# Block products (seven instead of eight) in the last matrix product of a fused attention and MLP kernel, with lam moved into W2

## The chip, the cores and the metric

The kernel runs on one core of a Trainium2 chip. A core has five engines with a queue each, worked through in order: TensorE (PE; its weight loads are listed apart, as PEld), VectorE (DVE), ScalarE (ACT), GpSimd (POOL) and SyncE (SP, which here only issues transfers). The engines meet at semaphores. SBUF is the working memory; PSUM, of eight banks, is where TensorE writes its sums. The metric is the device time of one execution in microseconds (us), the median of several runs.

## What is computed

The reference gives attention within blocks after a learned mixing of the blocks, and then a residual MLP. Batch 4, 8 heads, 768 rows, head size 64, 8 blocks of 96 rows, so C = 512 channels; hidden size 2048.

```python
P = sort_net                                   # (4, 8, 8, 8); five rounds of
P = exp(P - max);  P = P / rowsum;  P = P / colsum
k_sorted = einsum('bhij,bhjcd->bhicd', P, k_b) # v likewise
attn = softmax(q_b @ k_sorted^T / 8)           # within each block of 96 rows
x = attn @ v_sorted                            # then heads side by side: (4, 768, 512)

a1  = alpha1 * x + beta1
tok = einsum('ts,bsd->btd', w_tok, a1)
u   = x + lam * tok
a2  = alpha2 * u + beta2
ch  = relu(a2 @ w_ch1) @ w_ch2
out = u + lam * ch
```

## The kernel before

**Stages.** Everything is written out as one order of instructions for each engine (the class `Engine`, whose `fixed` keeps the order of the program on its engine). After a start-up for batch 0, a loop runs over the four batches b and over two halves hf of 384 rows each. I write such a half as (b, hf). A half has two phases:

- the **h phase**: sixteen units h0 to h15. A unit (`h_unit`, lines 725 to 741) is four matmuls of 128x384 that make 128 hidden rows of `a2 @ w_ch1`, and one ScalarE relu into `hTa` (m below 12) or `hTb`.
- the **c phase**: three output tiles kk = 0 to 2 of 128 rows and 512 columns, each in four parts of four matmuls (`ch_unit`, lines 760 to 780): twelve parts, c0 to c11. VectorE multiplies a finished tile by `lamB` (line 777), GpSimd adds `u` (line 778; VectorE in the last half), and two transfers write it out. The very last tile is split into 256, 128 and 128 columns (`last_out`, line 743).

**Work put between.** The table `at` (line 859) holds what is run after each unit or part: `put(b, hf, "h", m, f)` puts f after unit m. In the stretch of batch p the attention of batch p + 1 is put there (lines 882 to 927):

- `mix_v` and `mix_k` (lines 535 and 550) mix the blocks of the next values and keys on TensorE, and ScalarE or VectorE copies them out. `bounce_v` and `back_v` send the values through DRAM into `Vs`.
- `q_cross` (line 515) transposes the queries by transfers.
- `score` (line 419), for one head pair and one half of the blocks: eight small matmuls into a PSUM tile, and one ScalarE exp of 96x768 (`et`). Units go in pairs, written s0,s1 and so on to s6,s7.
- `pv` (line 479): eight matmuls into a PSUM tile `x_ps`, then on VectorE a reciprocal (`rcb`) and a multiplication into `x`. The two operations that make `a1` (`first_affine`, line 443) go to the list `late`, and `flush` (line 506) issues them. Pairs are written pv0,pv1 to pv6,pv7.
- `mix_matrix` (line 376) makes the mixing matrices of a later batch: one small matmul (`repv_ps`) and six VectorE operations, of which the first (`sel`) reads that PSUM tile.
- `moe_tok` (line 698): six matmuls of 128x512 (`tok_ps`), VectorE's multiplication by lam into `toktmp` and `u16`, and `u32` on GpSimd. `moe_cross` transposes `u16` by transfers, and `moe_affine` makes `a2T` from it.

**Buffers.** PSUM has two pools. `psA` has two buffers (of two banks) for `score`, `pv`, `mix_v`, `mix_k` and `mix_matrix`; `psB` has four buffers (of one bank) for `h_ps`, `ch_ps` and `tok_ps`. Each pool hands its buffers out in turn: a tile waits until the one that had its buffer (two tiles back in `psA`, four in `psB`) has been read. So TensorE waits where the reader of such a tile is late.

**Batch 0.** In (0,0) `w_tok` is still being transposed: `prep_wtok(ks, 1)` runs after unit ks, and its copy is VectorE's for even ks and ScalarE's for odd ones (line 871). `first_affine` for batch 0 runs after units 0 to 3 (line 877) and `moe_tok(0, 3 .. 5)` after units 7 to 9 (line 869).

Of the kernel before, what the change touches and what calls it, by code (L numbers as in the profile page):

```python
# [16 lines left out]
def kernel(  # L17
# [87 lines left out]
    lam1 = att.tile([1, C], FT, name="lam1", tag="toktmp", bufs=2)  # L105
    bet1 = att.tile([1, C], FT, name="bet1", tag="ost", bufs=2)
    nc.sync.dma_start(lam1[:], moe_lam.rearrange("(o c) -> o c", o=1))
    nc.sync.dma_start(bet1[:], moe_beta1.rearrange("(o c) -> o c", o=1))

    KT0 = att.tile([128, H4, NB, 128], F16, name="kT0", tag="kT", bufs=2)  # L110
    VD = att.tile([128, D, 64], F16, name="vd", tag="kT", bufs=2)
    Vs = [const([128, H * NB, GRP], F16, f"Vs_{n}") for n in range(2)]
    q8 = moep.tile([128, H4, 12 * D], F16, name="q8", tag="u16", bufs=1)
# [39 lines left out]
    for half in range(2):  # L153
        t_ = att.tile([128, 3, S], F16, name="wt16", tag=("mixed", "qn")[half], bufs=1)
        for lo, n in ((0, 96), (TAIL, 32)):
            pool.dma_start(
                t_[lo // 6:lo // 6 + n],
                moe_w_tok[lo + 3 * half * n:lo + 3 * (half + 1) * n, :].rearrange("(tt p) s -> p tt s", p=n),
            )
        wt16.append(t_)  # L160
        if half == 0:
            pool.memset(VD[:, :, HB:64], 0.0)
            pool.memset(
                KT0[:].rearrange("p g i (th t) -> p (g i th) t", th=2)[:, :, HB:64].bitcast(FT), 0.0
            )
# [4 lines left out]
    W1p = const([128, CT, HID], BF, "W1p")  # L170
    W2p = const([128, HT, C], BF, "W2p")
    w1v = moe_w_ch1.rearrange("(ci p) n -> p ci n", p=128)
# [230 lines left out]
    def v_mix(b, n, ps, eng):  # L403
        ps = ps([128, 8, 64], FT, "v_ps")
        fill(ps[:].rearrange("p d x -> p (d x)"), 1 - n % 2)
        for s in range(8):
            for th in range(2):
                d = (s + 4 * th) % 8
                r = slice(th * 64, th * 64 + 64)
                pe.matmul(  # L410
                    ps[r, d, :], VD[r, n * 8 + d, :],
                    bigV[b][r, :, :].rearrange("p h i -> p (h i)"), start=True, stop=True,
                )
        eng(Vs[0][:, :, n * 8:(n + 1) * 8], ps[:].rearrange("p d x -> p x d"))

# [3 lines left out]
    def score(b, g, hf, ps):  # L419
# [3 lines left out]
        for ii in range(4):  # L423
# [3 lines left out]
            for h2 in range(2):  # L427
# [4 lines left out]
                )  # L432
        tag, bufs = (("ost", "toktmp")[hf], 2) if (b, g) == (0, 3) else ("et", 6)
        et = att.tile([128, 2, 4, BLK], F16, name="et", tag=tag, bufs=bufs)
# [18 lines left out]
    def pv_first(g):  # L453
        if g == 0:
            x_of[0] = moep.tile([128, 8, C], F16, name="x128", tag="x128", bufs=2)
        ps = psa([128, 2, 512], FT, "x_ps")[:, :, 0:480].rearrange("p a (k d) -> p a k d", d=80)
        for i in range(NB):
            for h2 in range(2):
                et = ets[(0, g, i // 4)][:].rearrange("p a i t -> p (a i t)")
                lo = (4 * h2 + i % 4) * BLK  # L460
                w = min(128, 8 * BLK - lo)
                val = Vs[0][:, (2 * g + h2) * NB + i, 0:D + 1]
                if i < 6:
# [15 lines left out]
    def pv(b, g, hf):  # L479
        if g == 0 and hf == 0:  # L480
            x_of[b] = moep.tile([128, 8, C], F16, name="x128", tag="x128", bufs=2)
            a1_of[b] = moep.tile([128, 8, C], F16, name="a1", tag="a1", bufs=1)
        ps = psa([128, 2, 512], FT, "x_ps")[:].rearrange("p a (k d) -> p a k d", d=128)
        et = ets[(b, g, hf)][:].rearrange("p a i t -> p (a i t)")
        for ii in range(4):
            for h2 in range(2):
                lo = (4 * h2 + ii) * BLK
                w = min(128, 8 * BLK - lo)
                pe.matmul(
                    ps[0:w, h2, ii, 0:D + 1], et[0:BLK, lo:lo + w],  # L490
                    Vs[b % 2][0:BLK, (2 * g + h2) * NB + 4 * hf + ii, 0:D + 1], start=True, stop=True,
                )
# [13 lines left out]
    def flush():  # L506
        while late:
            late.pop(0)()

    def tails(x, lo, hi, eng):  # L510
# [24 lines left out]
    def mix_v(b, n, eng):  # L535
        if n == 0:
            mixed[b] = att.tile([128, HB, D], F16, name="mixed", tag="mixed", bufs=1)
        ps = psa([128, 2, 512], FT, "mix_ps")
# [37 lines left out]
    def back_v(b):  # L576
        sp.dma_start(Vs[b % 2][0:BLK, :, 0:D], vscr[b].rearrange("x t d -> t x d"))

# [136 lines left out]
    def moe_affine(b, hf):  # L715
        for ci in range(CT):
            affine(b, hf, ci, uT_of[(b, hf)][:, ci, :], dve)

    uT_of = {}

    hT_of = {}

    h_of = {}

    def h_part(b, hf, m, cis):
        if (b, hf) not in hT_of:
            hTa = moep.tile([128, 12, 384], BF, name="hTa", tag="hTa", bufs=1)
            hTb = moep.tile([128, HT - 12, 384], BF, name="hTb", tag="hTb", bufs=1)
            hT_of[(b, hf)] = [hTa[:, m, :] if m < 12 else hTb[:, m - 12, :] for m in range(HT)]
        if cis[0] == 0:  # L730
# [11 lines left out]

    def last_out(hT, cps, kk, kt):
        for n, (lo, hi) in enumerate(((0, 256), (256, 384), (384, 512))):
            c = slice(lo, hi)
            w = hi - lo
            if n:
                cps = psb([128, w], FT, "ch_ps")
                for m in range(HT):
                    pe.matmul(  # L750
                        cps[:], hT[m][:, kk * 128:(kk + 1) * 128], W2p[:, m, c],
                        start=(m == 0), stop=(m == HT - 1),
                    )
            ost = att.tile([128, C // 2], FT, name="ost", tag=("toktmp", "ost")[n % 2], bufs=2)
            dve.tensor_tensor(ost[:, 0:w], cps[:, 0:w], lamB[:, c], ALU.mult)
            dve.tensor_tensor(ost[:, 0:w], ost[:, 0:w], u_of[B - 1][kt][:, c], ALU.add)
            sp.dma_start(out[B - 1, kt * 96:(kt + 1) * 96, c], ost[0:96, 0:w])
            nc.scalar.dma_start(out[B - 1, TAIL + kt * 32:TAIL + (kt + 1) * 32, c], ost[96:128, 0:w])

    def ch_unit(b, hf, kk, part=(0, HT)):  # L760
# [4 lines left out]
        cps = ch_of[0]  # L765
        w = C // 2 if b == B - 1 and kt == NT - 1 else C
        for m in range(*part):
            pe.matmul(
                cps[:, 0:w], hT[m][:, kk * 128:(kk + 1) * 128], W2p[:, m, 0:w],
                start=(m == 0), stop=(m == HT - 1),  # L770
            )
        if part[1] < HT:
            return
        if b == B - 1 and kt == NT - 1:
            return last_out(hT, cps, kk, kt)
        ost = att.tile([128, C], FT, name="ost", tag="ost", bufs=2)
        dve.tensor_tensor(ost[:], cps[:], lamB[:], ALU.mult)
        (dve if b == B - 1 and hf == 1 else pool).tensor_tensor(ost[:], ost[:], u_of[b][kt], ALU.add)
        act_out(out[b, kt * 96:(kt + 1) * 96, :], ost[0:96, :])
        act_out(out[b, TAIL + kt * 32:TAIL + (kt + 1) * 32, :], ost[96:128, :])  # L780

    ch_of = {}
# [10 lines left out]
    prep_scales()  # L793
    dve.tensor_copy(Vs[0][:, :, D:GRP], mgap[:].unsqueeze(2).to_broadcast([128, H * NB, GRP - D]))
    kp0 = k_turn(0, 0, psb)
# [59 lines left out]
    load_q(1)  # L855
    pool.memset(Vs[1][0:BLK, :, D:GRP], 1.0)
    pool.memset(Vs[0][0:BLK, :, D:GRP], 1.0)

# [23 lines left out]
    for b in range(1, B):  # L882
        p = b - 1
        if b == 1:
            for n in range(3):
                put(0, 0, "h", 13 + n, lambda n=n: mix_v(1, n, dve.tensor_copy))
                put(0, 0, "c", 3 + 3 * n, lambda n=n: mix_k(1, n, ((act.copy, dve.tensor_copy)[n % 2],) * 4))
            put(0, 0, "h", 15, lambda: bounce_v(1))
# [8 lines left out]
        else:  # L897
# [9 lines left out]
            for (kind, n), at_ in zip(  # L907
                pairs, ((0, "h", 15), (0, "c", 1), (0, "c", 3), (0, "c", 6), (0, "c", 8), (0, "c", 11), (1, "h", 1), (1, "h", 4)),
            ):
                if kind == "p":  # L910
                    put(p, at_[0], at_[1], at_[2] + 1, flush)
                for i in range(2):
                    f = (lambda b=b, n=n + i: score(b, n // 2, n % 2, psa)) if kind == "s" else (lambda b=b, n=n + i: pv(b, n // 2, n % 2))
                    put(p, *at_, f)
        put(
            p, 1, "h", 15 if b == 1 else 8, lambda b=b: tails(a1_of[b], 0, C, dve.tensor_copy),
            lambda b=b: tails(x_of[b], 0, C, dve.tensor_copy),
        )
        put(p, 1, "h", 4, lambda b=b: moe_start(b))
        for kt in range(3):  # L920
            put(p, 1, "c", 4 if b == 1 else kt, lambda b=b, kt=kt: moe_tok(b, kt, psb))
        put(p, 1, "c", 4 if b == 1 else 2, lambda b=b: moe_cross(b, 0))
        put(p, 1, "c", 8 if b == 1 else 6, lambda b=b: moe_affine(b, 0))
        for kt in range(3):
            put(b, 0, "h", 2 * kt, lambda b=b, kt=kt: moe_tok(b, 3 + kt, psb))
        put(b, 0, "h", 4, lambda b=b: moe_cross(b, 1))
        put(b, 0, "c", 4, lambda b=b: moe_affine(b, 1))

# [11 lines left out]
    for b in range(B):  # L940
        for hf in range(2):
            for m in range(HT):
                if b or hf or m > 2:
                    h_unit(b, hf, m)
                    run(b, hf, "h", m)
            for kk in range(3):
                for part in range(4):
                    ch_unit(b, hf, kk, (4 * part, 4 * part + 4))
                    run(b, hf, "c", 4 * kk + part)

# [29 lines left out]
```

## Time and profile before

| what | value |
|---|---|
| median of 3 runs | 263.56 us (263.21 to 263.74) |
| the profiled execution | 263.49 us, of it a span of 261.7 us from the first to the last instruction |
| TensorE clock granted | 0.999 of full |
| waits of TensorE listed by the table of waits | 4.5 us, the longest of them 1.2 us |
| idle time of VectorE until a `ch_ps` tile was done | 54.6 us in 16 waits |
| idle time of ScalarE until an `h_ps` tile was done | 53.8 us in 75 waits |
| GpSimd adding `u` to output tiles | 26.6 us busy, 21 times, 1268 ns each |

One table by stage reads busy time in each stretch of the span (us). The stretches are (1,0), (1,1), (2,0), (2,1), (3,0) and (3,1), cut where a phase or an attention pair ends:

| stretch | length | PE | DVE | ACT | POOL |
|---|---|---|---|---|---|
| 102.4 to 130.6 | 28.2 | 28.20 | 14.66 | 14.34 | 13.34 |
| 130.6 to 158.9 | 28.3 | 28.30 | 17.90 | 18.75 | 11.74 |
| 158.9 to 186.8 | 27.9 | 27.90 | 13.43 | 14.23 | 8.78 |
| 186.8 to 212.5 | 25.7 | 25.70 | 16.16 | 9.10 | 8.74 |
| 212.5 to 237.1 | 24.6 | 24.60 | 8.33 | 7.84 | 8.78 |
| 237.1 to 261.7 | 24.6 | 21.01 | 5.48 | 7.84 | 1.27 |

A listed matmul time includes its drain and overlaps the next, so the cost of a matmul is read from the distance between starts, not from the busy time of one.

### The profile page before, as it was taken

The page shows a single profiled execution, that of the slowest core. Times are in us where ns is not written, and L with a number is a line of the kernel's source. Part 1 is how long each engine was busy: PE and PEld are TensorE (multiplying, and loading weights), DVE is VectorE, ACT ScalarE, POOL GpSimd, SP SyncE. Part 2 cuts the span into 40 slices and gives each one's busy share as a digit, 9 for nine tenths or more (in the row PEclk, how much of TensorE's full clock was granted, in tenths as well). Part 3 has the DMA queues.
Part 4 walks back from the last instruction along what each step waited for, and adds up shares of the span by engine and source line. Part 5 has one row for each costly group of instructions (what it writes and reads, how often), then busy time and mean ns, then how long its engine had stood idle before and what let it go on. Part 6 is the DMA issues. An engine that isn't in the chain of part 4 may idle for free.

```text
span 261.7 us, 5406 instructions
## 1 busy us (share of the span) xinstructions
PE 253.1 (97%) x2179; PEld 140.2 (54%) x2179; DVE 153.8 (59%) x345; ACT 133.8 (51%) x242; POOL 100.2 (38%) x105
## 2 busy tenths in 40 slices
PE   8998799999999999999999999999999999999994
PEld 3456565555556455555565454555565445545554
DVE  6796857987658984613988643407894554051024
ACT  3568666224787539474276288573373014504700
POOL 8759304501382084612860554501302746032000
PEclk9999999999999999999999999999999999999999
DMA  6999999998979957960899859901110332112012
GB/s 101 208 206 186 206 207 213 204 147 188 159 152 183 133 125 181 130 108 3 167 178 179 121 122 170 135 20 40 46 38 0 63 93 67 23 40 80 0 43 80
DMA packets 67533, 31.04 MB, mean 119 GB/s; under 512 B 56675, under 2 KB 63219, under 8 KB 67509
## 3 DMA queue, kind: packets, MB, share of 16 engines
q0 software_dynamic: 26352, 15.34, 42.3%
q1 hardware_dynamic: 41012, 15.30, 34.3%
q8 instruction: 17, 0.28, 0.4%
q10 hardware_dynamic: 144, 0.07, 0.1%
q14 instruction: 8, 0.06, 0.1%
HBM read 32.79 MB, written 8.65 MB: 158 GB/s over the span
## 4 chain that ended last, share of the span: by engine, by line
PE 82%; DMA 10%; POOL 5%; DVE 2%; issue 1%; ACT 0%; POOLq 0%
PE ch_ps L65 32%; PE h_ps L65 30%; PE tok_ps L65 10%; DMA W2p<-in_moe_w_ch_dram 6%; DMA v<-in_v_dram 4%; PE x_ps L65 2%; PE sc_ps L65 2%; DVE a L65 2%; PE kmix_ps L65 2%; PE mix_ps L65 1%; POOL W1p L65 1%; POOL vd L65 1%; POOL k L65 1%; PE qt_ps L65 1%; POOL brow L65 0%
## 5 line engine op out<-in xcount | busy, mean ns | idle before, releaser
L65 PE MATMUL h_ps<-a2T,W1p 128*128 128x384 bf16 x512 | 91.8, 326 | 0.1
L65 ACT ACTIVATE hTa<-h_ps 128x384 bf16<-128x384 f32 x96 | 46.7, 493 | 54.0 <-PE h_ps L65 53.8
L65 PE MATMUL ch_ps<-W2p,hTa 128*128 128x512 bf16 (+2 forms) x312 | 69.0, 363 | 0.0
L65 PEld LDWEIGHTS <-W1p 128*128 128x128 bf16 x512 | 48.3, 98 | 32.3 <-issue 0.3
L65 POOL TENSOR_TENSOR ost<-ost,u 128x512 f32<-128x512 f32 x21 | 26.6, 1268 | 80.2 <-DVE ost L65 53.2
L65 DVE TENSOR_TENSOR ost<-ch_ps,lamB 128x512 f32<-128x512 f32 (+2 forms) x26 | 16.8, 648 | 54.6 <-PE ch_ps L65 54.6
L65 PEld LDWEIGHTS <-hTa 128*128 128x128 bf16 x312 | 28.7, 98 | 28.9
L65 POOL TENSOR_TENSOR u<-toktmp,x 128x512 f32<-128x512 f32 x18 | 29.6, 1650 | 32.1 <-DVE toktmp L65 32.1
L65 ACT ACTIVATE et<-sc_ps 96x768 f16<-96x768 f32 (+1 forms) x32 | 24.8, 808 | 18.9 <-PE sc_ps L65 18.9
L65 PE MATMUL tok_ps<-a,w_tokT 128*128 128x512 f16 x126 | 30.3, 379 | 0.1
L65 ACT CAST kT<-kmix_ps 64x512 f16<-64x512 f32 x32 | 22.9, 717 | 10.1 <-PE kmix_ps L65 9.8
L65 DVE TENSOR_TENSOR toktmp<-tok_ps,lamB 128x512 f32<-128x512 f32 x21 | 14.5, 690 | 20.0 <-PE tok_ps L65 18.6
L65 PE MATMUL ch_ps<-W2p,hTb 128*128 128x512 bf16 (+2 forms) x104 | 25.0, 363 | 0.0
L65 PEld LDWEIGHTS <-w_tokT 128*128 128x128 f16 x126 | 12.2, 98 | 14.0 <-DVE a L65 0.5
L65 ACT ACTIVATE hTb<-h_ps 128x384 bf16<-128x384 f32 x32 | 15.7, 490 | 7.5 <-PE h_ps L65 7.2
L65 POOL DMA_DIRECT2D qn<-in_q_dram x18 | 16.0, 910 | 6.4 <-DMA raw<-in_v_dram 6.4
L65 DVE TENSOR_TENSOR u<-toktmp,x 128x512 f16<-128x512 f32 (+1 forms) x24 | 17.0, 719 | 0.7
L65 DVE TENSOR_TENSOR x<-x_ps,rcb 96x512 f16<-96x512 f32 x24 | 16.5, 687 | 0.8
L65 PEld LDWEIGHTS <-et 96*128 96x128 f16 (+4 forms) x288 | 11.9, 100 | 5.5 <-DVE x L65 1.6
L65 PEld LDWEIGHTS <-hTb 128*128 128x128 bf16 x104 | 9.6, 98 | 9.6
L65 PE MATMUL x_ps<-Vs,et 96*128 96x65 f16 (+4 forms) x288 | 13.0, 195 | 1.7 <-DVE x L65 0.9
L65 DVE TENSOR_TENSOR a<-x,alphaB 96x512 f16<-96x512 f16 (+1 forms) x28 | 13.8, 491 | 0.0
(118 smaller groups left out, 230.1 us busy)
## 6 DMA issues: line engine op xcount, KB each, us to landing
out_dram<-ost SPq DMA_DIRECT2D x23, 192.0 KB, 2.3
raw<-in_v_dram POOLq DMA_DIRECT2D x6, 384.0 KB, 8.1
raw<-in_k_dram POOLq DMA_DIRECT2D x6, 384.0 KB, 9.9
qn<-in_q_dram POOLq DMA_DIRECT2D x18, 128.0 KB, 11.0
vscr<-mixed SPq DMA_DIRECT2D x6, 384.0 KB, 5.2
Vs<-vscr SPq DMA_DIRECT2D x3, 768.0 KB
W1p<-in_moe_w_ch_dram POOLq DMA_DIRECT2D x4, 512.0 KB, 11.5
W2p<-in_moe_w_ch_dram POOLq DMA_DIRECT2D x4, 512.0 KB, 17.3
```

Source lines behind the costliest of these rows:

```text
L65: ins = getattr(self.eng, name)(*args, **kwargs)
```

## The change

1. **Block products.** In batches 1 to 3 tile 0 of each half stays as it was, and tiles 1 and 2 are made together by `ch_pair`. Rows, hidden size and columns are each cut in two, so there would be eight products of 128x1024 by 1024x256; seven suffice, each of eight matmuls of 128x256. Three sums of the hidden rows (`block_sums`) and four of the weights (`block_weights`) replace the eighth. Three PSUM tiles px, py, pz hold the running sums and are read between the products: VectorE adds their parts into the outputs in eight operations of 128x256 (`add_out`). In the last half the pair comes first and tile 0 last, in 256, 128 and 128 columns.
2. **lam in W2.** `scale_weights` multiplies 64 lam into W2 in four VectorE operations (128x2048 each) in (0,0); an output is then one VectorE operation, `ps / 64 + u`. GpSimd's additions to the outputs are gone.
3. **Types and buffers.** W2, `hTa` and `hTb` are f16 instead of bf16 and hold eight units each; four `ost` buffers instead of two; one `Vs` and one `x128` instead of two; `mixed` shares a buffer with the sums, or for batch 3 with `qn`.
4. **Places.** The pairs of `score` and `pv` move from h15, c1, c3, c6, c8, c11 and h1, h4 of the next half to h7, h10, h12, h15, c1, c4, c10 and h1. `first_affine` is flushed at h13, c6, c8 and h3. `moe_tok(b, 0 .. 2)` for b above 1 moves from c0, c1, c2 to h13, h14, h15. For b = 1, `mix_v` and `mix_k` are copied by ScalarE alone. `moe_affine(b, 1)` moves to ScalarE for b of 1 and more.

The core of the diff:

```diff
@@ h_part, ch_unit, new functions @@
+            hTa, hTb = (
+                moep.tile([128, HK, 384], F16, name=n, tag=n, bufs=1) for n in ("hTa", "hTb")
+            )
...
-        ost = att.tile([128, C], FT, name="ost", tag="ost", bufs=2)
-        dve.tensor_tensor(ost[:], cps[:], lamB[:], ALU.mult)
-        (dve if b == B - 1 and hf == 1 else pool).tensor_tensor(ost[:], ost[:], u_of[b][kt], ALU.add)
+        ost = att.tile([128, C], FT, name="ost", tag="ost", bufs=4)
+        add_out(ost[:], cps[:], u_of[b][kt])
...
+    def scale_weights(g):
+        if g == 0:
+            lam16 = lam_of[0] = att.tile([128, C], F16, name="lam16", tag="ost", bufs=4)
+            dve.tensor_scalar(lam16[:], lamB[:], GAIN, 0.0, op0=ALU.mult, op1=ALU.add)
+        w = W2p[:, 4 * g:4 * g + 4, :]
+        dve.tensor_tensor(w, w, lam_of[0][:].unsqueeze(1).to_broadcast([128, 4, C]), ALU.mult)
+
+    def add_out(dst, ps, other):
+        dve.scalar_tensor_tensor(dst, ps, 1.0 / GAIN, other, op0=ALU.mult, op1=ALU.add)
...
+        dst, x, y = ((t1, b12, b11), (t2, b22, t1), (t3, b22, b12), (t4, b21, t2))[n // 2]
+        dve.tensor_tensor(dst, x, y, ALU.subtract)
...
+    def block_sums(b, hf, part, k1=1, k2=2):
...
+        r = slice(part * HK // 2, (part + 1) * HK // 2)
+        dve.tensor_tensor(sm[:, 0, r, :], ha[:, r, c2], hb[:, r, c2], ALU.add)
+        dve.tensor_tensor(sm[:, 1, r, :], sm[:, 0, r, :], ha[:, r, c1], ALU.subtract)
+        dve.tensor_tensor(sm[:, 2, r, :], hb[:, r, c1], sm[:, 1, r, :], ALU.subtract)
+        if part:
+            dve.tensor_tensor(ha[:, :, c2], ha[:, :, c1], ha[:, :, c2], ALU.subtract)
...
+        px = psb([128, c], FT, "px")[:]
+        product(px, lambda j: ha[:, j, c1], lambda j: W2p[:, j, left], True)
+        o1 = att.tile([128, C], FT, name="ost", tag="ost", bufs=4)
+        add_out(o1[:, left], px, u1[:, left])
+        step()
+        py = psb([128, c], FT, "py")[:]
+        product(py, lambda j: hb[:, j, c1], lambda j: W2p[:, HK + j, left], True)
+        add_out(o1[:, left], py, o1[:, left])
...
+        step()
+        pz = psb([128, c], FT, "pz")[:]
+        product(pz, lambda j: sm[:, 0, j, :], lambda j: TW["a"][:, 0, j, :], True)
+        o2 = att.tile([128, C], FT, name="ost", tag="ost", bufs=4)
+        add_out(o2[:, right], pz, u2[:, right])
+        step()
+        product(px, lambda j: sm[:, 1, j, :], lambda j: TW["a"][:, 1, j, :], False)
+        add_out(o1[:, right], px, u1[:, right])
+        step()
+        product(pz, lambda j: sm[:, 2, j, :], lambda j: W2p[:, HK + j, right], False)
+        add_out(o1[:, right], pz, o1[:, right])
...
+        step()
+        product(py, lambda j: hb[:, j, c2], lambda j: TW["b"][:, 1, j, :], True)
+        add_out(o2[:, left], py, u2[:, left])
+        step()
+        product(px, lambda j: ha[:, j, c2], lambda j: TW["b"][:, 0, j, :], False)
+        for n, d in enumerate((right, left)):
+            add_out(o2[:, d], px, o2[:, d])
...
@@ places @@
-                pairs, ((0, "h", 15), (0, "c", 1), (0, "c", 3), (0, "c", 6), (0, "c", 8), (0, "c", 11), (1, "h", 1), (1, "h", 4)),
+                pairs, ((0, "h", 7), (0, "h", 10), (0, "h", 12), (0, "h", 15), (0, "c", 1), (0, "c", 4), (0, "c", 10), (1, "h", 1)),
...
+            put(p, 0, "h", 13, flush)
+            put(p, 0, "c", 6, flush_one)
+            put(p, 0, "c", 8, flush_one)
+            put(p, 1, "h", 3, flush)
...
+    for g, m in enumerate((3, 12, 13, 14)):
+        put(0, 0, "h", m, lambda g=g: scale_weights(g))
+    for n, at_ in enumerate(((0, 1, "h", 13), (0, 1, "h", 14), (0, 1, "h", 15), (0, 1, "c", 11)) + tuple((1, 0, "h", 5 + i) for i in range(4))):
+        put(*at_, lambda n=n: block_weights(n))
+    for b in range(1, B):
+        for hf in range(2):
+            put(b, hf, "h", 11, lambda b=b, hf=hf: block_sums(b, hf, 0))
+            put(b, hf, "h", 15, lambda b=b, hf=hf: block_sums(b, hf, 1))
...
+            for kk in range(1 if b else 3):
                 for part in range(4):
                     ch_unit(b, hf, kk, (4 * part, 4 * part + 4))
-                    run(b, hf, "c", 4 * kk + part)
+                    step()
+            if b:
+                ch_pair(b, hf, step)
+                step()
```

Each `step()` runs the work put at the next c place, so in batches 1 to 3 c0 to c3 follow the parts of tile 0 and c4 to c10 follow the seven products.

## Prediction, written before the result was known

> **What bounds the kernel now.** First the page's busy shares and the chain that ended last:
>
> ```profile
> span 261.7 us, 5406 instructions
> ...
> PE 253.1 (97%) x2179; PEld 140.2 (54%) x2179; DVE 153.8 (59%) x345; ACT 133.8 (51%) x242; POOL 100.2 (38%) x105
> ...
> PE 82%; DMA 10%; POOL 5%; DVE 2%; issue 1%; ACT 0%; POOLq 0%
> ```
>
> From some 44 us on the chain is TensorE's own queue; the other engines wait for it. TensorE's waits, of the table of waits, are as good as none in the loop (all lie in the start-up), so nothing there can be won but its own work:
>
> ```profile
> PE x_ps L65 <- DVE x L65: 0.9, 2, 0.4
> ...
> PE sc_ps L65 <- ACT et L65: 0.3, 1, 0.3
> ```
>
> Then the timeline, for the price of a matmul by its columns (start, length, and here the distance between starts), and for the spacing on ScalarE and VectorE:
>
> ```profile
> 250.96 2.75 PE L65 MATMUL ch_ps<-W2p,hTa 128*128 128x512 bf16 x12
> ...
> 254.41 1.47 PE L65 MATMUL ch_ps<-W2p,hTa 128*128 128x256 bf16 x12
> ...
> 256.16 0.83 PE L65 MATMUL ch_ps<-W2p,hTa 128*128 128x128 bf16 x12
> ```
>
> ```profile
> 173.38 0.49 ACT L65 ACTIVATE hTb<-h_ps 128x384 bf16<-128x384 f32 x1 [0.16 <-PE h_ps L65]
> 173.77 1.50 ACT L65 ACTIVATE et<-sc_ps 96x768 f16<-96x768 f32 x2
> ...
> 178.55 0.19 DVE L65 RECIPROCAL rcb<-x_ps 96x8 f32<-96x8 f32 x1
> ...
> 178.78 0.69 DVE L65 TENSOR_TENSOR x<-x_ps,rcb 96x512 f16<-96x512 f32 x1
> ```
>
> A tile of sixteen 512-column matmuls takes 254.41 - 250.96 = 3.45 (215.6 ns each), of 256 columns 256.16 - 254.41 = 1.75 (109.4 ns), and each loads its own weights; six f16 matmuls of `tok_ps` start 1.30 before what follows them, so f16 is as fast as bf16. ScalarE follows a relu with an exp after 0.39, an exp with the next after 0.69; relu's result is there 0.49 after its start, exp's 0.81. A relu starts 0.20 after its last matmul. A `pv` tile holds VectorE for 0.24 + 0.61, and is read 0.93 after `rcb` starts.
>
> **What is won.** Two tiles cost 32 x 215.6 = 6.90; seven products 56 x 109.4 = 6.13. 0.77 by six pairs: **-4.6**. At the end one operation stands for two of 0.29 behind the last matmul; the nearest form (SCALAR_TENSOR_TENSOR, 128x384, 618 ns) against TENSOR_TENSOR on the slope 292, 424, 690 ns makes it some 0.35: **-0.2**. GpSimd's 26.6 us were behind TensorE and win nothing.
>
> The Trainium skill, page "TensorE: Matmul & The Clock Gate", section "Back-to-back issue gap", speaks against the change: it says that in a stream of weight load and matmul both set the spacing, measured at 81 ns for 128 columns and 131 ns for 512. An estimate from it by a straight line (98 ns at 256) makes a pair 5.5 instead of 4.2 us, 7.8 lost over six pairs. The rows above (55.6, 109.4, 215.6 ns) are proportional to the columns, and they decide.
>
> **What VectorE gets.** 16-bit TENSOR_TENSOR from SBUF takes 0.42 at 512 and 0.55 at 768 (0.53 ns an element), so 0.42 for 512, 0.69 for 1024, 1.23 for 2048. The other end is the slope of the 32-bit rows, 1.04 ns: 0.69, 1.22, 2.28. I take the first, since those rows are of the same kind, with a broadcast operand too. `add_out` at 256: 0.42 (TENSOR_TENSOR) to 0.62 (the 384 row), taken as 0.48. Per half: sums 6 x 0.42 + 0.69 = 3.2 and nine additions 4.6, for three multiplications of 0.69. VectorE stays under TensorE in sum; what counts is what stands behind what.
>
> **Where TensorE will wait.** I followed the queues unit by unit, time t from h0 of a half; an h unit is 0.65, a `moe_tok` 1.30, a score pair 0.45, a `pv` pair 0.51.
>
> (0,0). The copy of `prep_wtok(4)` was at 44.02 and `moe_tok(0,3)` began at 44.16. lam16 (0.65) and the first W2 piece (1.23) now stand before that copy: done at 46.2, wanted by the fifth matmul at 45.0. **+1.2**. The other three pieces take the place of the `mixed` copies that go to ScalarE (3.48), and end some 59.3, while their parts of the first tile begin from 57.6 to 60.2: hidden, at nothing unless the 2.28 price holds.
>
> (0,1). VectorE has no pause from 76 to 91 there. Three `block_weights` (spacing 0.6) delay the `a1` tails, needed at 91.2 and done at 90.35, by two of them, 1.2: +0.5. The third `kT` group on ScalarE delays the next relus: +0.2. **+0.7**.
>
> (1,0). With s0,s1 at h7 and s2,s3 at h10, ScalarE runs relu7 9.29, exp 9.68 and 10.37, relus 11.06, 11.45, 11.84, exp 12.23 and 12.92, relu11 13.61, done 14.10. `block_sums` part 0 waits for relu11 and stands first on VectorE: 14.16 to 15.40. Behind it `sel` of `mix_matrix(3)`: 15.62. pv0 needs the buffer of s3 (13.8 instead of 13.4); pv1 needs that of `repv_ps`, which `sel` reads: 15.7 instead of 14.06. 2.0 lost. The same VectorE queue gives x0 and x1 late, whose buffers s4 and s5 want at 17.9: x1 ends 18.44, +0.4. pv6 at h1 of the next half needs pv4's and pv5's buffers; pv4 now ends only 1.3 before (c10), two tiles cost VectorE 1.7 behind px's two additions: +0.8. **+3.2**.
>
> (2,0). No `mix_matrix`; pv1 waits for s3's exp (13.8 for 13.5), +0.3. x0 stands behind the sums, 15.64 to 16.33, x1 ends 17.17; s4 and s5 want these buffers at 16.0 and 16.2: +1.0. pv6 as above +0.8. **+2.1**.
>
> Within the pair: pz is written again one product (0.875) after its first, and its reading takes 0.20 + 0.48 + 0.07: just in time while VectorE is free. It costs nothing beyond (c6 and c8 put 0.8 of `first_affine` between, and the places where the reader is late had slack of two products).
>
> Behind the pair. The next half's second `psB` tile gets px's buffer, free 0.2 + 0.42 + 0.48 + 0.07 = 1.17 after the last product; h0 covers 0.65. (3,0) to (3,1): +0.5. (1,1) to (2,0): +0.5. (2,1) to (3,0): `a2T`'s four operations (1.25) stand before py's addition: +0.85. After (1,0) and (2,0) the pv pair covers it. **+1.9**.
>
> Beside GpSimd. One 16-bit `a` on VectorE took 2.06 instead of 0.41, ending as two GpSimd additions did:
>
> ```profile
> 133.29 2.50 POOL L65 TENSOR_TENSOR ost<-ost,u 128x512 f32<-128x512 f32 x2
> ...
> 134.02 2.06 DVE L65 TENSOR_TENSOR a<-x,alphaB 96x512 f16<-96x512 f16 x1
> ```
>
> So in (b,1) I let part 1 of the sums wait 1.0 for the last `u32` of `moe_tok`; it is then done 1.6 before pz's product wants it, which hides it. Without that cover the 1.0 would be lost in (1,1) and (2,1).
>
> Queues that are passed: GpSimd's loads for the next batch keep c4 and have no additions ahead of them; SP issues `Vs<-vscr` of batch 3 one output later, some 2 us into (2,0) instead of 0.9; the pv of (2,0) comes at 13.2, so the transfer (768 KB; the slices after its issue at 105.2 moved 130 GB/s, about 6 us) lands some 5 us before. `mixed` of batch 3 waits for the last `qT` transposes (last issue ended 145.9, landing 4.0; the copy is due about 17.9 into (1,1), 148.5): 0 to 0.5, taken as 0.
>
> **Sum.** -4.6 - 0.2 + 1.2 + 0.7 + 3.2 + 2.1 + 1.9 = +4.3 on the span of 261.7: 266.0; 1.8 lie around the span (263.49 - 261.7), and the profiled execution is 0.07 under the median. **267.8**.
>
> **Rivals.** What this kernel's measurement can tell from no change is 0.2%, 0.5 us.
> - *Buffers come free in time* (faster). The 7.2 of (1,0), (2,0) and behind the pair are one mechanism: PSUM buffers whose reader stands behind other work. If TensorE finds them free, 267.8 - 7.2 = 260.6. For it: the waits before are nearly none, and VectorE is 52% busy in (1,0). Against: the order on VectorE is fixed, and relu11 cannot start before the exps in front. It decides once these waits cost under 2.9 instead of 7.2. 0.23.
> - *VectorE at the slow slope* (1.04 ns): W2's first piece +1.05, the last piece 2.2 late for its part, sums 0.8 and the difference 0.7 later in (1,0) and (2,0): +6.2, 274. Against: the 768 row. 0.06.
> - *Break-even*: these waits at 2.4 to 3.4: 0.07.
> - *The products are no cheaper*: at 123 ns a matmul (6.90 / 56) the 4.6 are gone, 272.4. The 109.4 with a weight load each speaks against: 0.04.
>
> **Numbers.** Forecast 0.60, with its own range 265.5 to 269.5 (each of the nine waits summed here to 9.1 is good to some 0.3, and they lean together). Faster 0.23, within 0.2% 0.07, slower 0.70. To hold 8 in 10 the range takes in part of the first rival and little of the slow ones: 261.5 to 270.5.
>
> **What would show it.** 128x256 `px`, `py`, `pz` matmuls at 109 ns apart; TensorE waits of some 2 us at pv1 in (1,0), for VectorE's `sel`; of 1 us at s4,s5 in (2,0), for x; of 0.5 to 0.9 at the second `psB` tile after a pair; 1.2 at `tok_ps` near 45 us. Busy time of TensorE down by some 4 us while its idle time grows by twice that. If those waits sum to under 2.9 us, or `block_sums` does not hold `rcb` back, the prediction is wrong.

## The result, and the profile after

The changed kernel takes 275.21 us (median of four runs, 273.43 to 278.60), the kernel before beside it 263.65: a ratio of 1.041, 95% interval 1.032 to 1.050. It is slower, as forecast, but by 11.6 us and not by 4.2, and outside the range. (Ratios and intervals here leave out an execution that is more than 1.5% above the fastest of its kernel, of these four the one of 278.60.) The profiled execution took 276.55 us. First its page, the lines that answer to those of before: the span, the busy shares and the chain that ended last.

```profile
span 274.4 us, 5761 instructions
...
PE 252.7 (92%) x2323; PEld 155.7 (57%) x2323; DVE 180.0 (66%) x412; ACT 145.4 (53%) x261; POOL 73.3 (27%) x83
...
PE 63%; DMA 9%; ACT 5%; DVE 4%; issue 1%; SPq 0%; DVEq 0%
```

TensorE is busy for 252.7 us, as before (253.1), in a span 12.7 longer. And the chain of work that ended last, which was TensorE's own queue from 44 us on, now goes through two transfers in the loop: `Vs<-vscr` is 6% of it and `vscr<-mixed` 3%. (The 10% of transfers in the chain of before were loads of weights and values in the start-up.) The table of TensorE's waits (engine and tile, released by what; us in total, times, longest) says where:

```profile
PE x_ps L65 <- DMA Vs<-vscr: 9.0, 1, 9.0
PE x_ps L65 <- DVE x L65: 1.7, 4, 0.4
PE x_ps L65 <- DVE sel L65: 1.5, 1, 1.5
...
PE sc_ps L65 <- DVE x L65: 1.0, 3, 0.5
...
PE tok_ps L65 <- DVE w_tokT L65: 0.8, 1, 0.8
```

Lines two to five are, but for two waits of 0.43 us in the start-up that the kernel before has too, waits that the prediction named. The first is not in it: one wait of 9.0 us, longer than all the others together. TensorE's timeline around it (start, length, instruction, idle time before it and what ended that):

```profile
74.24 0.82 PE L65 MATMUL h_ps<-a2T,W1p 128*128 128x384 bf16 x4
84.04 0.62 PE L65 MATMUL x_ps<-Vs,et 96*128 96x65 f16 x8 [8.97 <-DMA Vs<-vscr]
84.48 1.47 PE L65 MATMUL h_ps<-a2T,W1p 128*128 128x384 bf16 x4
```

It is pv0 of batch 1, after h3 of (0,1), and it waits for the values that go through DRAM into `Vs`. What follows runs slowly too: four h matmuls take 1.47 instead of 0.82. The windows of the same trace show why (stretch, then busy time of each engine, and in the third column from the right the granted TensorE clock):

```profile
79.00:80.00 1.00, 0.00 (x0) 0.00 (x0) 0.00 (x0) 0.00 (x0) 0.00 (x0) 1.00 2.01 145
80.00:81.00 1.00, 0.00 (x0) 0.00 (x0) 0.00 (x0) 0.00 (x0) 0.00 (x0) 0.55 2.01 144
...
89.00:90.00 1.00, 1.00 (x11) 0.76 (x10) 0.95 (x3) 0.45 (x1) 0.00 (x0) 0.50 0.00 0
90.00:91.00 1.00, 1.00 (x12) 0.44 (x10) 0.94 (x3) 0.14 (x2) 0.00 (x0) 0.83 0.00 0
```

Five microseconds after TensorE went idle its clock fell to half, and it stayed there until 90.3, six after work had come back. The Trainium skill, page "TensorE: Matmul & The Clock Gate", section "Part 1: The HAM clock gate", has such a gate: it shows a fall 5.2 us after the last matmul, near which this trace lies (5.0), and a return after some 3.4 us of work, where this trace has 6.3.

The chain of waits in the stretch of 55 to 92 us gives the two transfers ahead of that wait (start, length, what):

```profile
59.88 8.58 DMA vscr<-mixed
...
68.52 15.39 DMA Vs<-vscr
```

Before, SP issued `vscr<-mixed` at 58.06 and `Vs<-vscr` at 64.33. Windows of half a microsecond of that trace (the last column is what the transfers moved, in GB/s) show that the traffic ended at 72.0, before pv0 at 73.50:

```profile
71.50:72.00 0.50, 0.50 (x11) 0.33 (x11) 0.00 (x0) 0.50 (x2) 0.50 (x2) 1.00 0.45 164
72.00:72.50 0.50, 0.50 (x4) 0.17 (x2) 0.00 (x0) 0.50 (x2) 0.50 (x2) 1.00 0.00 0
```

What else is on the transfer engines is seen in GpSimd's timeline, first of the kernel before, then of the changed one:

```profile
70.75 1.26 POOL L65 TENSOR_TENSOR ost<-ost,u 128x512 f32<-128x512 f32 x1 [0.91 <-DVE ost L65]
71.96 1.09 POOL L65 DMA_DIRECT2D raw<-in_v_dram  x2
73.03 1.05 POOL L65 DMA_DIRECT2D raw<-in_k_dram  x2
```

```profile
58.10 1.07 POOL L65 DMA_DIRECT2D raw<-in_v_dram  x2 [6.79 <-PE mix_ps L65]
68.98 1.03 POOL L65 DMA_DIRECT2D raw<-in_k_dram  x2 [9.81 <-PE kmix_ps L65]
70.51 5.30 POOL L65 DMA_DIRECT2D qn<-in_q_dram  x6 [0.51 <-PE qt_ps L65]
```

Before, the loads of batch 2 stood behind three additions to the output tiles of (0,0) in GpSimd's queue, and the last of these ended at 72.0. The additions are gone, so the values' load (two transfers of 384 KB) is issued 13.9 us earlier, as soon as its buffer is free, beside `vscr<-mixed`; keys and queries (768 KB each) are issued beside `Vs<-vscr`, which itself has 768 KB. That is a reading of two traces, and the first experiments test it.

For the rest, the length of each stretch, from the start of h0 to the start of the next h0 (last one: to the end of the span), worked out from TensorE's timelines. The last three columns are experiments that follow.

| stretch | before | changed | loads held | all places mended | the same, no products |
|---|---|---|---|---|---|
| to (0,1) | 69.72 | 70.91 | 70.92 | 70.46 | 69.98 |
| (0,1) | 32.73 | 44.83 | 33.08 | 32.95 | 32.95 |
| (1,0) | 28.12 | 29.95 | 29.95 | 28.43 | 28.70 |
| (1,1) | 28.32 | 27.62 | 27.62 | 27.00 | 27.80 |
| (2,0) | 27.88 | 28.83 | 28.81 | 28.32 | 28.46 |
| (2,1) | 25.69 | 24.99 | 24.98 | 24.37 | 25.16 |
| (3,0) | 24.65 | 23.85 | 23.86 | 23.85 | 24.64 |
| (3,1) | 24.62 | 23.45 | 23.45 | 23.44 | 24.28 |
| span | 261.7 | 274.4 | 262.7 | 258.8 | 262.0 |

Of the 12.7 us on the span, (0,1) alone has 12.1. Outside it the change costs 0.6.

### The profile page after: what moved, and what is told of

It is laid out like the page before. It is cut to its first block, busy times and chain, and to the rows that moved or that the text cites. A ratio compares the mean times of both kernels' runs of the same rounds, so it can differ in the third digit from the quotient of the medians.

```text
span 274.4 us, 5761 instructions
## 1 busy us (share of the span) xinstructions
PE 252.7 (92%) x2323; PEld 155.7 (57%) x2323; DVE 180.0 (66%) x412; ACT 145.4 (53%) x261; POOL 73.3 (27%) x83
## 4 chain that ended last, share of the span: by engine, by line
PE 63%; DMA 9%; ACT 5%; DVE 4%; issue 1%; SPq 0%; DVEq 0%
PE h_ps L65 23%; PE ch_ps L65 11%; PE tok_ps L65 10%; PE px L65 6%; DMA Vs<-vscr 6%; PE py L65 4%; PE pz L65 4%; DMA vscr<-mixed 3%; DVE x L65 2%; ACT hTb L65 2%; PE x_ps L65 2%; ACT et L65 2%; PE sc_ps L65 1%; ACT mixed L65 1%; PE kmix_ps L65 1%; DVE sums L65 1%
## 5 line engine op out<-in xcount | busy, mean ns | idle before, releaser
L65 PE MATMUL h_ps<-a2T,W1p 128*128 128x384 bf16 x512 | 95.2, 331 | 0.1
L65 ACT ACTIVATE hTa<-h_ps 128x384 f16<-128x384 f32 x64 | 31.1, 492 | 54.8 <-PE h_ps L65 54.8
L65 ACT ACTIVATE hTb<-h_ps 128x384 f16<-128x384 f32 x64 | 30.8, 495 | 23.1 <-PE h_ps L65 22.7
L65 PEld LDWEIGHTS <-hTa 128*128 128x128 f16 x208 | 19.4, 98 | 10.9
L65 PEld LDWEIGHTS <-hTb 128*128 128x128 f16 x208 | 19.2, 98 | 10.2
L65 PE MATMUL ch_ps<-W2p,hTb 128*128 128x512 f16 (+2 forms) x112 | 23.9, 349 | 0.0
L65 PE MATMUL ch_ps<-W2p,hTa 128*128 128x512 f16 (+2 forms) x112 | 23.6, 349 | 0.0
L65 DVE TENSOR_TENSOR sums<-hTa,hTb 128x512 f16<-128x512 f16 x12 | 7.0, 582 | 21.0 <-ACT hTb L65 20.9
L65 PEld LDWEIGHTS <-w_tokT 128*128 128x128 f16 x126 | 12.1, 98 | 14.7 <-DVE w_tokT L65 1.3
L65 DVE RECIPROCAL rcb<-x_ps 96x8 f32<-96x8 f32 x24 | 4.7, 197 | 16.5 <-PE x_ps L65 16.5
L65 PEld LDWEIGHTS <-sums 128*128 128x128 f16 x144 | 14.0, 98 | 1.6
```

Source lines behind the costliest of these rows:

```text
L65: ins = getattr(self.eng, name)(*args, **kwargs)
```

## The experiments

Theory A: GpSimd's loads for batch 2, let loose by the removal of its additions, slow the two transfers of batch 1's values. Theory B: `Vs` is late by itself, through its one buffer, the later copies of `mixed` and SP's order.

**Loads held.** GpSimd copies one element that relu0 of (0,1) writes, and issues the loads after it.

```diff
+    gate = const([1, 1], F16, "gate")
+    def hold(m):
+        pool.tensor_copy(gate[:], hT_of[(0, 1)][m][0:1, 0:1])
...
-            put(0, 0, "c", 11, lambda: load_kv(2), lambda: load_q(2))
+            put(0, 1, "h", 0, lambda: hold(0), lambda: load_kv(2), lambda: load_q(2))
```

> The changed kernel, with GpSimd's loads for batch 2 held until the first relu of (0,1) by a one-element copy that reads it (some 72.5 us into the span, as in the kernel before; 58.1 in the changed one). Theory A (these loads, released early because GpSimd's additions are gone, slow vscr<-mixed and Vs<-vscr on the shared transfer engines): vscr<-mixed takes at most 6 us instead of 8.6, Vs<-vscr is issued near 65 and has landed before pv0 wants it near 75; TensorE's 9.0 us wait and the half clock after it are gone; 263 to 265 us. Theory B (Vs<-vscr is late by the one Vs buffer, the later copies of mixed and the order on SP, whatever GpSimd loads): the wait stays at 5 us or more, the time above 270.

Measured: 265.3 us (264.78 to 266.0, 8 runs) against 264.01 of before; ratio 1.0053, interval 1.0037 to 1.0069. GpSimd and SP in its timeline:

```profile
73.13 0.18 POOL L65 COPY gate<-hTa 1x1 f16<-1x1 f16 x1 [21.65 <-ACT hTa L65]
73.64 1.07 POOL L65 DMA_DIRECT2D raw<-in_v_dram  x2 [0.33 <-PE sc_ps L65]
```

```profile
59.32 1.15 SPq L65 DMA_DIRECT2D vscr<-mixed  x2
...
65.10 0.33 SPq L65 DMA_DIRECT2D Vs<-vscr  x1
```

With the loads at 73.6, `Vs<-vscr` is issued at 65.10 instead of 68.52, TensorE waits for no transfer in (0,1), the clock is 0.999, and (0,1) has 33.08 us instead of 44.83. `Vs` still has one buffer, and `mixed` is sent at 59.32 as in the changed kernel (59.31). So theory B does not hold. A median 0.3 above what was expected remains.

**The same edit's effect in the kernel before.** Only the three additions of (0,0) move to VectorE; two `Vs` buffers, no products, no lam in W2.

```diff
-        (dve if b == B - 1 and hf == 1 else pool).tensor_tensor(ost[:], ost[:], u_of[b][kt], ALU.add)
+        (dve if (b, hf) in ((0, 0), (B - 1, 1)) else pool).tensor_tensor(ost[:], ost[:], u_of[b][kt], ALU.add)
```

> The kernel before, with one edit: the three additions of u to the output tiles of (0,0) go from GpSimd to VectorE, so that GpSimd's loads for batch 2 have nothing before them. Two Vs buffers, no products, lam not in W2. Theory A: the loads start near 58 instead of 72, Vs<-vscr lands late, TensorE waits 5 to 9 us at pv0 of (0,1), and the clock falls to half for some us: 269 to 275 us. Theory B: 263 to 265 us, no wait over 1 us.

Measured: 276.94, 277.20, 277.94 and 271.43 us, against 264.01. The fastest lost 7.4 us, the other three some 13; the profiled one is of the three (277.20). Of its table of waits and of TensorE's timeline:

```profile
PE x_ps L65 <- DMA Vs<-vscr: 11.4, 1, 11.4
```

```profile
72.95 0.82 PE L65 MATMUL h_ps<-a2T,W1p 128*128 128x384 bf16 x4
85.19 0.62 PE L65 MATMUL x_ps<-Vs,et 96*128 96x65 f16 x8 [11.42 <-DMA Vs<-vscr]
85.63 1.47 PE L65 MATMUL h_ps<-a2T,W1p 128*128 128x384 bf16 x4
```

Its loads start at 57.00 (values) and 67.91 (keys); `vscr<-mixed` takes 9.76 and `Vs<-vscr` 16.47 us. (0,1) has 46.34 us instead of 32.73, the other stretches are as before. So one small edit to a fast kernel, which takes work off an engine that nobody waits for, brings the same wait and the same half clock. The fastest execution lies in the range that was expected, the others above it; why they differ is not shown, since only one was traced.

**Which load slows which transfer.** The values' load goes early, only keys and queries are held.

```diff
+            put(0, 0, "c", 11, lambda: load_kv(2, ((1, v),)))
+            put(0, 1, "h", 0, lambda: hold(0), lambda: load_kv(2, ((0, k),)), lambda: load_q(2))
```

> As the run with all loads held, but the values' load (raw<-in_v of batch 2, issued at 58.1) goes early and only keys and queries are held. If the values' load is what slows vscr<-mixed, and the keys and queries what slows Vs<-vscr: Vs<-vscr is still issued at 67 to 68.5, but lands in 6 to 9 us instead of 15.4, so TensorE waits 0 to 3 us and the clock does not fall; 264 to 267 us. If the values' load does all the harm: 270 or more. If it does none: as the run with all held, within 0.5 us.

Measured: 266.28 us (265.33 to 271.73, 4 runs), ratio 1.0084, interval 1.0052 to 1.0117. The chain of waits shows both transfers:

```profile
59.63 8.19 DMA vscr<-mixed
67.87 7.54 DMA Vs<-vscr
```

The values' load makes `vscr<-mixed` long (8.19; issued at 59.05, with its successor issued at 67.87, where all loads held gave 59.32 and 65.10). Keys and queries double `Vs<-vscr` (7.54 to 15.39). TensorE waits 0.8 us in the profiled execution, the fastest of the four, and the clock stays at 1.0: there most of the loss is keys and queries beside `Vs`. The execution of 271.73 had a mean clock of 0.987, so the values' load alone may at times cost more; it was not traced. The Trainium skill, page "DMA: Bandwidth & Descriptors", section "Queues, rings and completion order", says that each transfer engine takes turns between the queues it has work for; a transfer that doubles beside another queue's load agrees with it.

**What the products win, in these places.** As loads held, but three tiles of sixteen 512-column matmuls, no `block_sums`, no `block_weights`.

```diff
-            for kk in range(1 if b else 3):
+            for kk in range(3):
...
-            if b:
-                ch_pair(b, hf, step)
-                step()
```

> As the run with all loads held, but without products: all three tiles of each half by sixteen matmuls of 512 columns, no block_sums and no block_weights. All else of the change stays. Compared with the run with all loads held: if seven products save the 4.6 us that the matmul spacing gives (0.77 a pair) and the sums and additions cost TensorE about 3 us of waits in (1,0) and (2,0), this run is 1 to 3 us slower than that one. If the products save nothing net, it is equal or faster. Expected 264.5 to 267 us.

Measured: 265.2 us (264.8 to 267.42, 10 runs), as good as with products. From (0,1) on its profiled span has 192.4 us, with products 191.7: they win about 0.7 net in the trace and nothing that the medians show. (Its profiled execution lost 1.75 in the start-up; more of that at the end.) The expected 1 to 3 us came out as 0 to 0.7.

**Sums behind the reader.** Loads held, and part 0 of `block_sums` after h13 in the first halves.

```diff
-            put(b, hf, "h", 11, lambda b=b, hf=hf: block_sums(b, hf, 0))
+            put(b, hf, "h", 11 if hf else 13, lambda b=b, hf=hf: block_sums(b, hf, 0))
```

> The run with the loads held, and part 0 of block_sums in the first half of each batch put after h13 instead of h11, so that VectorE reads the mixing matrix and the pv tiles of h12 first. If the predicted waits are real and are those of readers behind the sums, TensorE's 1.5 us wait for sel in (1,0) and its 0.8 us for x at s4,s5 in (2,0) go: 2 us less than the run with the loads held, 263 to 263.8 us. If ScalarE's exps or something else set these places, the time is within 0.5 us of that run.

Measured: 264.07 us (263.44 to 265.1, 10 runs) against 263.92; ratio 0.9985, interval 0.9961 to 1.0008: 1.2 us under loads held by the medians, and 1.8 by the two ratios (0.0068 of 264). The wait for `sel` is gone, and (1,0)'s h phase is 17.19 instead of 18.78. But in the execution that was profiled, the slowest of the ten, its c phase lost 1.45 of these 1.6 again. Half of that is VectorE's: both parts of the sums now stand together before the `x` of pv2 and pv3, and TensorE waits for these at s6 and s7, which it did not with the loads held:

```profile
126.71 0.34 PE L65 MATMUL sc_ps<-qT,kT 64*128 64x96 f16 x8 [0.23 <-DVE x L65]
127.54 0.35 PE L65 MATMUL sc_ps<-qT,kT 64*128 64x96 f16 x8 [0.49 <-DVE x L65]
```

Then TensorE waits for `a2T`, 1.2 us in four waits from the first h unit of (1,1) on. ScalarE's timeline:

```profile
133.32 2.50 ACT L65 ACTIVATE a2T<-uT,ab2col 128x384 bf16<-128x384 f16 x4 [4.52 <-DMA uT<-u]
```

`a2T` came at 133.3 instead of 129.6, because SP's transposes `uT<-u`, issued at 114.05, were in issue for 8.62 us instead of 4.41. GpSimd's loads for batch 3 are issued at 114.05 too, but with the loads held they come at 113.78, beside transposes issued at 112.78; that they are the cause is not shown. So the wait that was predicted is real, and part of what its removal wins is lost again at the next reader.

**The first W2 piece later.** Loads held, and `scale_weights(0)` after h5.

```diff
-    for g, m in enumerate((3, 12, 13, 14)):
+    for g, m in enumerate((5, 12, 13, 14)):
```

> The run with the loads held, and lam16 and the first W2 piece after h5 instead of h3, behind VectorE's copy of w_tokT that TensorE waits for near 45 us. If that copy is the whole of the (0,0) loss, 1.2 us less than the run with the loads held, 264 to 264.3 us; if the work only meets the next reader, no change.

Measured: 265.0 us (263.5 to 265.83, 10 runs), ratio 1.0025, interval 0.9997 to 1.0053. In the trace the wait is gone: from the first `tok_ps` (44.79) to c0 (57.04) it has 12.25 us, with loads held 13.25 (44.40 to 57.65), before 12.24. The medians show only 0.3 to 0.7 of that 1.0, and the runs spread over 2.3 us, more than the effect. The spread goes with the clock of each execution: the six of the ten with a mean granted clock of 0.987 to 0.994 took 264.77 to 265.83, the four with 0.998 or more 263.5 to 264.36. Those four have a mean of 264.0, the five of loads held with such a clock 265.15, so like beside like shows 1.1.

**All places mended.** Both of these edits, and `mix_matrix(3)` after h3, pv4 and pv5 after c8, three `block_weights` in the c phase of (0,1).

```diff
-    put(1, 0, "h", 12, lambda: mix_matrix(3))
+    put(1, 0, "h", 3, lambda: mix_matrix(3))
...
-                pairs, ((0, "h", 7), (0, "h", 10), (0, "h", 12), (0, "h", 15), (0, "c", 1), (0, "c", 4), (0, "c", 10), (1, "h", 1)),
+                pairs, ((0, "h", 7), (0, "h", 10), (0, "h", 12), (0, "h", 15), (0, "c", 1), (0, "c", 4), (0, "c", 8), (1, "h", 1)),
...
-    for n, at_ in enumerate(((0, 1, "h", 13), (0, 1, "h", 14), (0, 1, "h", 15), (0, 1, "c", 11)) + tuple((1, 0, "h", 5 + i) for i in range(4))):
+    for n, at_ in enumerate(((0, 1, "c", 6), (0, 1, "c", 9), (0, 1, "c", 10), (0, 1, "c", 11)) + tuple((1, 0, "h", 5 + i) for i in range(4))):
```

> All places mended at once: loads held; block_sums part 0 after h13; the first W2 piece after h5, behind the copy of w_tokT; mix_matrix(3) after h3 of (1,0); pv4,pv5 after c8 instead of c10; the first three block_weights after c6, c9 and c10 of (0,1). From the waits in the trace with the loads held: 1.2 (w_tokT) + 1.5 (sel) + 0.2 and 0.8 (s4,s5) + 2 x 0.6 (pv6,pv7) less about half an us for what moves elsewhere: 4 to 5 us under that run, 260 to 261.5 us, faster than the kernel before.

Measured: 260.44 us (260.0 to 260.93) against 263.92; ratio 0.985, interval 0.980 to 0.990. This version is faster than both kernels, by 1.5% than the one before. Its page:

```profile
span 258.8 us, 5761 instructions
...
PE 249.6 (96%) x2323; PEld 154.8 (60%) x2323; DVE 180.6 (70%) x412; ACT 145.1 (56%) x261; POOL 73.8 (29%) x84
```

TensorE is at 96% again, with 3.5 us less work than before (253.1). Of the waits for VectorE in the loop one of 0.35 us is left in (1,0), and one like it in (2,0).

**The same without products.** Places as there, tiles as in the run without products.

> The run with all places mended, without products: three tiles of sixteen 512-column matmuls in each half, no block_sums, no block_weights. The difference to the run with products is what they win once TensorE waits for nothing: 6 x 0.77 = 4.6 us by the matmul spacing, so 264 to 266 us. If the products still cost waits, the difference is under 3 us.

Measured: 263.96 us (263.39 to 264.82, 10 runs), ratio 0.9998, interval 0.9975 to 1.002: products win 3.5 us once their sums delay little, where the matmul spacing promised 4.6. The table by stretch shows the rest: 0.79 to 0.84 for a pair in (1,1), (2,1), (3,0) and (3,1), but 0.27 and 0.14 in (1,0) and (2,0). In each of these two the wait of 0.35 for `x` explains more than half of what is missing; the rest is not accounted for. Without products the kernel takes as long as the one before: in these places lam in W2 and the rest of the change win nothing by themselves.

**Batch 3's loads held as well, beside a second measurement.** The loads go behind relu11 of (1,0).

```diff
-                put(p, 0, "c", 4, lambda b=b: load_kv(b + 1), lambda b=b: load_q(b + 1))
+                put(p, 0, "h", 11, lambda b=b: hold(11, b - 1, 0), lambda b=b: load_kv(b + 1), lambda b=b: load_q(b + 1))
```

> The run with all places mended, and GpSimd's loads for batch 3 held in the same way: until relu11 of (1,0), some 3 us later, since in one trace SP's transposes uT<-u of (1,1), issued at 114, were slowed beside these loads (issued at 114) and a2T came 1.2 us late. If that collision still costs in the mended kernel, 0.3 to 1 us less than it, and less spread; if it only met that one execution, the same within 0.3 us; if the later loads make qT or mixed of batch 3 late, 0.5 to 2 us more.

> The kernel with all places mended once more, beside the run that also holds batch 3's loads, and for a second measurement of its gain on the kernel before: 260 to 261 us, ratio 0.985 to 0.99.

Measured: 260.36 us (ratio 0.9846, interval 0.982 to 0.987) and, for the mended kernel again, 260.59 (0.9857, 0.983 to 0.988). The same within 0.3, with intervals that overlap: slow transposes `uT<-u` are not what this kernel pays for. The gain on the kernel before is confirmed, 1.4 to 1.5%.

## Why the prediction was wrong, point by point

- **The step that failed:** "GpSimd's 26.6 us were behind TensorE and win nothing", and with it the sentence that GpSimd's loads "keep c4 and have no additions ahead of them", which was costed at nothing. The additions did no work that TensorE waited for, but they held the loads of batch 2 back until 71.96, while batch 1's values travelled until 72.0 at the latest. That the two times meet is luck of the kernel before. The prediction looked at the loads put at c4 and at `Vs<-vscr` of batch 3 alone. Batch 2's loads at c11 of (0,0) and `Vs<-vscr` of batch 1 were in none of its sums. Cost: 44.83 - 33.08 = 11.75 us in (0,1), of it 9.0 waiting and the other 2.8 while the clock was at half. This is shown by holding the loads (the loss goes) and by freeing them in the kernel before (it comes).
- **The rest of the sum was too high.** It had +4.3 on the span; with the loads held the span grew by 1.0. The direction would have been right by 0.5% only. The waits of (1,0) and (2,0), priced at 5.3, lost 4.3 by the stretches (with 0.77 won a pair), of which the table of waits lists 3.3; those behind the pair, priced at 1.9, lost nothing.
- **Behind the pair, +1.9: wrong, nothing there.** The rule, given in the section on the kernel before as well, was that buffers of `psB` come in turn, so that h1 gets px's. In (3,0) px's last two readings run from 251.18 to 251.94, while h1 runs at 250.98 + 0.65 = 251.63, with no gap in the 64 matmuls from 250.98 to 261.38. So h1 doesn't have px's buffer. The order of the instructions has h1, h2 and h3 each waiting for a VectorE operation of its own, which fits buffers given back in the order of their last readers. That reading was not tried by itself.
- **(0,0), +1.2: right in place, 1.0 in size** (13.25 against 12.24 us), shown by the trace with the later W2 piece. **(0,1), +0.7:** 0.35 (33.08 against 32.73).
- **(1,0), `sel` behind the sums, 2.0: right, 1.5.** VectorE's timeline of the changed kernel shows the order that was predicted, sums from 129.87, `sel` at 131.12, and TensorE's pv1 at 131.39 (the line below). TensorE waited 0.2 at s5 for a predicted 0.4, and 0.4 at pv7 for 0.8. **(2,0):** it waited 0.30 and 0.49 at s4 and s5, for 1.0; 0.4 at pv7, for 0.8; and not at pv1, for 0.3.

```profile
131.39 0.41 PE L65 MATMUL x_ps<-Vs,et 96*128 96x65 f16 x8 [1.47 <-DVE sel L65]
```

- **The spacing and the products, -4.6: right.** Seven products start 0.87 to 0.88 apart, as these two lines show, and a pair wins 0.79 in (2,1) and (3,0) once all places are mended:

```profile
249.24 1.04 PE L65 MATMUL py<-TWb,hTb 128*128 128x256 f16 x8
250.11 1.04 PE L65 MATMUL px<-TWb,hTa 128*128 128x256 f16 x8
```

- **VectorE's prices: right.** `sums` 0.42, `lam16` 0.42 (0.65 was taken), the first W2 piece 1.22 (1.23), `add_out` 0.42 at 256 columns (0.48 was taken). **Beside GpSimd: right.** In (1,1) and (2,1) the first operation of part 1 of the sums took 1.38 us instead of 0.42, beside GpSimd's `u` (162.71 and 219.17 us, GpSimd's from 162.15 and 218.60, 1.66 each): 0.96 longer, where 1.0 was predicted. TensorE did not wait for it, as predicted. **The tail, -0.2:** about -0.4, the last half wins 1.17 with the loads held, where (3,0) wins 0.79.
- **The rival "buffers free in time" (260.6) is not what happened**, though the mended kernel has nearly its time (260.44). It took all of 7.2 us of waits away, and was to decide if they cost under 2.9. In the changed kernel's own places, with the loads held, the table lists 3.3, and by the stretches 4.3 were lost. That the two times agree is luck: the mended kernel has other places, no wait in (0,0), and products that win 3.5 and not 4.6. No rival named the transfer.

## What to carry to other kernels

Work on an idle engine can be a gate: before it is taken away, look at what stands behind it in that queue, transfers above all, and at which critical transfer is in flight when these come free. In the trace of before, the end of `Vs<-vscr` at 72.0 and the start of the loads at 71.96 were the sign. Where a change adds operations to an engine that reads PSUM, put each behind the readings that TensorE waits for; here that, with the other moves, raised what the same products win from 0 to 0.7 us to 3.5.

## What the runs showed of the hardware that was not expected

- The stretches at half clock have lengths that are whole multiples of some 3.4 us. It was at half from 80.1 to 90.3 in the changed kernel (10.2 us), from 76.6 to 90.3 in the kernel before with early loads (13.7), from 29.9 to 33.3 in the run with loads held and no products (3.4), and from 22.6 to 26.0 in the second measurement of the mended kernel (3.4): three, four, one and one. It fell 5.0 us after TensorE's last matmul in the first, but 2.9 in the second.
- The length of a gap alone does not say whether the clock falls. In the third it fell in the start-up, 0.8 us after the end of a gap of 1.2 us; in the fourth within a gap of 1.5 us there. A wait of 1.5 us for `sel` in the loop did not bring it down, nor did gaps of 1.15 us in the start-up of the run with sums behind the reader and of the mended kernel's first trace. What decides is not shown. The lines of the third:

```profile
27.03 0.84 PE L65 MATMUL x_ps<-Vs,et 128*128 128x65 f16 x18 [0.43 <-DVE x L65]
29.08 0.34 PE L65 MATMUL x_ps<-Vs,et 128*32 128x65 f16 x6 [1.21 <-issue]
```

Nothing in the profile releases that wait. Eleven of the twelve traces have one at this place, of 0.4 to 1.2 us. Such falls of the clock are part of why single executions of one kernel here differ by 1 to 2 us: in the run with loads held and no products, the three of ten with a mean clock of 0.994 took 266.1 to 267.42, the seven with 0.998 or more 264.8 to 265.6.
